# A fused linear-attention and squared-ReLU kernel: fill-in matmuls, another layout of the second weight matrix, and paired products instead of a doubled first product

## The chip, the cores and the metric

The kernel runs on one core of one Trainium2 chip. That core has a matmul engine (TensorE, "PE" in the profile, with its weight loads shown apart as "PEld"), three engines for elementwise work (VectorE or "DVE", ScalarE or "ACT", GpSimd or "POOL"), and SyncE ("SP"), which here only issues transfers. Sixteen DMA engines move the data. The metric is the device time of one launch in microseconds, lower is better.

## The reference, cut to what matters

Four batches, eight heads, 768 steps, head size 48. Per head a state of 48 x 48 decays by `w` each step and takes in `k` outer `v`; the result then goes through a two-layer block with a squared ReLU.

```python
for t in range(S):                      # S = 768, per batch and head
    cur = u * k[t] (outer) v[t]
    y[t] = r[t] @ (state + cur)
    state = w * state + k[t] (outer) v[t]
x = y as [3072, 384]                    # batch*step rows, head*48 columns
h = x @ w_in                            # [384, 2048]
g = max(h, 0) ** 2
out = g @ w_out                         # [2048, 384]
```

## The kernel before, in words

The 768 steps are cut into six chunks of 128. A **unit** is one chunk of one batch, 128 rows of `x` with all eight heads; there are 24, numbered chunk first, so unit `i` needs the state that unit `i - 4` left. For one unit the work is:

1. Three loads `rt`, `kt`, `vt` (`load`, L288), each 128 rows by 8 heads by 48 floats, in pieces of 192 bytes, on SP's queue.
2. `scale` (L311, DVE): `r` times a rising and `k` times a falling power of the decay, in bf16. `cast_v` (L315, ACT) casts `v`.
3. Both scaled tensors are transposed. For units 0 to 6 (`NPE = 7`) this is done by PE (`turn`, L331) and an ACT copy out of PSUM (`evict_rk`, L335); for the others by one DMA transpose on SP's queue (`turn_dma`, L320).
4. `at` (L348, PE): eight products q k^T of 64 x 128 operands, one per head. `mask` (L360, DVE, two a unit) keeps the part above the diagonal.
5. `rk`, `sums`, `diag_v` (L340, L368, L373, L382): the `u` term, and k^T v for the state. `state_add`, `state_decay`, `state_cast` (L390 to L402) carry the state.
6. `y_mm` and `evict_y` (L411 to L426): the unit's `y`. It is transposed to `xT`, by PE and ACT (`x_turn` L442, `evict_x` L446) for units 0 to 5 (`NPY = 6`) and by a DMA transpose on SP's queue (`x_dma`, L435) for the others.
7. `mm1` (L458): the first big product. A step makes one PSUM bank of 512 columns; a unit has four steps `s`, each with four blocks of 128 rows of `w_in` columns and three matmuls a block. `GROUPS` says over how many units a step reaches: for single units the moving operand has 128 columns, for a pair of units 256. In the kernel before units 0 to 7 and 20 to 23 are single and units 8 to 19 go in six pairs.
8. `relu` (L466, ACT) out of PSUM, then `square` on ACT (L473) or DVE (L475), dealt out in turn by `SQUARES = 'AMM'`: one on ACT, two on DVE.
9. `mm2` (L482): sixteen matmuls with 384 moving columns in four quarters, `evict_o` (L489, ACT), `store` (L519, SP). The last unit does it in two halves (L497, L508, L510, L515).

The weights come in eight transfers, four quarters `I0` to `I3` of `w_in` and four quarters `O0` to `O3` of `w_out` (`weights`, L294 to L302), on POOL's queue, cast to bf16 as they land. Ahead of each stands a small copy that waits until the `kt` load of a named unit has landed (list `front`). `columns` (L255, L256) loads `w` and `u` once more, one column a head pair; `spread_columns` (L268, PE) and `copy_columns` (L271, DVE) turn them, and POOL makes from them the `u` matrix (L274, L277) and the decay over a chunk (`end_columns`, L280, L282).

**Order.** Every engine's instruction order is written out by a planner (`Plan.run`, L42). Each step has an engine, an assumed cost, what it needs, and a rank; the planner steps through an assumed time, and gives a free engine the step of lowest rank whose needs, buffers and PSUM bank are there. What it produces is a fixed order for each engine; on the chip each engine takes its instructions in that order and waits at each for what it needs. `L1 = 7` and `L2 = 16` are the rank distances of `mm1` and `mm2` behind the attention work of the same unit (four ranks a unit). `room` and the banks' table limit buffers. `at_pair` and the branches on `PAIRED` are there in the kernel before but `PAIRED` is empty.

Of the kernel before, what the change touches and what calls it, by code (L numbers as in the profile page):

```python
# [10 lines left out]
BF16 = mybir.dt.bfloat16  # L11
# [138 lines left out]
def kernel(  # L150
# [11 lines left out]
    nc = tc.nc  # L162
# [10 lines left out]
    NPY = 6  # L173
    NPAD = 4
    SQUARES = 'AMM'
    GROUPS = (1,) * 8 + (2,) * 6 + (1,) * 4
    PAIRED = ()

    const = ctx.enter_context(tc.tile_pool(name="const", bufs=1))
    loads = ctx.enter_context(tc.tile_pool(name="loads", bufs=6))  # L180
    work = ctx.enter_context(tc.tile_pool(name="work", bufs=4))
    xpool = ctx.enter_context(tc.tile_pool(name="xpool", bufs=3))
    gpool = ctx.enter_context(tc.tile_pool(name="gpool", bufs=2))
    mpool = ctx.enter_context(tc.tile_pool(name="mpool", bufs=8))
# [21 lines left out]
    nc.scalar.preload_act_table_set("natural_log_exp_and_others")  # L206
    wu = const.tile([HP, 2, 2, 64], F32)
# [40 lines left out]
    w_in_sb = const.tile([128, NK, dff], BF16)  # L248
    w_out_sb = const.tile([128, NF, dm], BF16)
# [4 lines left out]
    def columns():  # L254
        nc.sync.dma_start(out=wu[:, 0, :, :D], in_=w.rearrange("(p o) d -> p o d", o=2))  # L255
        nc.sync.dma_start(out=wu[:, 1, :, :D], in_=u.rearrange("(p o) d -> p o d", o=2))  # L256
# [36 lines left out]
    def weights(i, q, which):  # L293
        nc.gpsimd.tensor_copy(gate, tiles[i]["kt"][:, 0, :1])  # L294
        if which == "I":
            sl = slice(q * dff // NQ, (q + 1) * dff // NQ)
            src = moe_w_in.rearrange("(ko ki) f -> ki ko f", ki=128)
            nc.gpsimd.dma_start(out=w_in_sb[:, :, sl], in_=src[:, :, sl])
        else:
            sl = slice(q * NF // NQ, (q + 1) * NF // NQ)  # L300
            src = moe_w_out.rearrange("(ko ki) f -> ki ko f", ki=128)
            nc.gpsimd.dma_start(out=w_out_sb[:, sl, :], in_=src[:, sl, :])  # L302
# [145 lines left out]
    def mm1(i, m, s):  # L448
        c, b = units[i]
        t = tiles[i]  # L450
        if b == 0 and s == 0:
            chunks[c]["g"] = gpool.tile([128, NF, B, C], BF16, name="g")
        t["h", s] = bank("h", i, s).rearrange("p (a u c) -> p a u c", u=m, c=C)
        for a in range(4 // m):
            f = s * (4 // m) + a
            for n in range(NK):
                turned = w_in_sb[:, n, f * 128 : (f + 1) * 128]
                nc.tensor.matmul(  # L458
                    out=t["h", s][:, a], lhsT=turned, rhs=chunks[c]["xT"][:, n, b : b + m, :],
                    start=(n == 0), stop=(n == NK - 1),  # L460
                )
# [15 lines left out]
    def mm2(i, q):  # L477
        t = tiles[i]
        if q == 0:
            t["o"] = bank("o", i)[:, :dm]  # L480
        for f in range(q * 4, q * 4 + 4):
            nc.tensor.matmul(  # L482
                out=t["o"], lhsT=chunks[units[i][0]]["g"][:, f, units[i][1], :], rhs=w_out_sb[:, f, :],
                start=(f == 0), stop=(f == NF - 1),
            )
# [5 lines left out]
    def mm2_half(i, n):  # L491
# [4 lines left out]
        for f in range(NF):  # L496
            nc.tensor.matmul(  # L497
                out=t["o"][:, sl], lhsT=chunks[units[i][0]]["g"][:, f, units[i][1], :], rhs=w_out_sb[:, f, sl],
                start=(f == 0), stop=(f == NF - 1), skip_group_check=True,
            )  # L500
# [23 lines left out]
    L1, L2 = 7, 16  # L524
# [11 lines left out]
    copy("wu", SP, 1.46, columns, rank=-99.75, move=(0.1, 16, 0.67, 0.1))  # L536
# [3 lines left out]
    add("wend", POOL, 2.6, end_columns, rank=-90, needs=["copied"])  # L540
    front = ['U0', 'U1', 'I0', 'U2', 'U3', 'I1', 'I2', 'I3', 'O0', 'O1', 'O2', 'O3', 'U4', 'U5']
    place = {what: -100 + n for n, what in enumerate(front)}
    seen = -1
    for what in front:
        if what[0] == "U":
            seen = int(what[1:])
        else:
            q = int(what[1])
            copy(
                (what[0], q), POOL, 1.0, do(weights, seen, q, what[0]), rank=place[what], move=((2.35, 98, 1.25, 0.0) if what[0] == "I" else (2.5, 78, 1.25, 0.0)),  # L550
                needs=[("kt", seen)], uses=[("ld", seen)],
            )
    for i in range(NU):
# [3 lines left out]
        rank = place.get(f"U{i}", a - 24)  # L557
# [5 lines left out]
        for x in range(2):  # L563
# [6 lines left out]
            ("vb", i), ACT, 0.405, do(cast_v, i), rank=a + 0.5, needs=[("vt", i), ("rkT", i) if i < 24 else ("scale", i, 1)],  # L570
# [17 lines left out]
        if i in PAIRED:  # L588
            add(
                ("at", i), PE, 0.645, do(at_pair, i), rank=a + 0, needs=[("rkT", i), ("rkT", i + 1)],  # L590
# [6 lines left out]
        for o in range(2):  # L597
# [5 lines left out]
            ("sums", i), PE, 0.275 if c < NCH - 1 else 0.105, do(sums, i), rank=a + (2.1 if c else 3.1),  # L603
# [3 lines left out]
        add(("dv", i), DVE, 0.465, do(diag_v, i), rank=a + 2.9, needs=[("sums", i), ("vb", i)], new=[("dv", i)], uses=[("s", i), ("vb", i)])  # L607
        if c < NCH - 1:
            add(
                ("sadd", i), DVE, 0.68, do(state_add, i), rank=a + (6 if c else 3.2),  # L610
                needs=[("sums", i), ("stb", before) if c else "wend"], uses=[("s", i)],
            )
            if c > 0:
                add(("sdec", i), DVE, 0.27, do(state_decay, i), rank=a + 4 + 4, needs=[("sadd", i)])
            add(
                ("stb", i), ACT, 0.71, do(state_cast, i), rank=a + 6 + 4,
# [18 lines left out]
    for m in GROUPS:  # L635
# [3 lines left out]
        for s in range(4 * m):  # L639
            rank = 4 * i + s + L1 + 4 * (m - 1)  # L640
# [12 lines left out]
        for j in range(i, i + m):  # L653
            a = 4 * j
            squares = [[("sq", i, s) for s in range(q * m, q * m + m)] for q in range(NQ)]
            if j < NU - 1:
                for q in range(NQ):
                    add(
                        ("m2", j, q), PE, 0.652, do(mm2, j, q), rank=a + q + L2 + 4 * (m - 1),
# [18 lines left out]
        ld=6, rkw=NPAD, g=2, rkT=4, vb=4, rk=4, am=8, dv=4, yb=4, xT=3, gr=8, osb=8,  # L678
    )
    for s in plan.run(room, dict(at=4, s=2, y=2, h=4, o=2), len(banks)):  # L680
# [32 lines left out]
```

## Time and profile before

| | |
|---|---|
| median of 3 runs | 183.15 us (180.97 to 185.44) |
| profiled execution, device time | 179.87 us |
| its span, first to last instruction | 178.1 us |
| busy: PE / DVE / ACT / POOL | 163.5 / 144.8 / 118.8 / 12.4 us |
| weight loads on PE, beside its matmuls | 125.2 us |
| DMA queue of SP, of POOL, as a share of 16 engines' span | 79.7% / 11.0% |

The profile's page gives busy time by engine, the span in 40 slices, the DMA queues, the chain of work that ended last, and the costliest groups of instructions. A busy PE isn't PE at its full rate, since matmuls overlap each other and their ends are modelled; the rate is read from how long a run of like matmuls takes in the timeline or the chain. The profiled execution is 3.3 us below the median of the runs shown.

### The profile page before, as it was taken

What the parts mean: (1) busy time and instruction counts of PE and PEld (TensorE: products, weight loads), DVE (VectorE), ACT (ScalarE), POOL (GpSimd) and SP (SyncE); (2) the same over time, 40 slices, a digit from 0 to 9 for tenths busy, and PEclk for the clock granted to TensorE, in tenths of its full rate; (3) what the DMA queues carried; (4) which work ended last, traced back from release to release, by engine and by line L of the source; (5) the groups of instructions that cost most, each with busy time, mean ns of one, the idle gap of its engine ahead of it and who ended that gap; (6) DMA issues with size and microseconds to landing.
All of it is one profiled execution on the core that took longest, in us unless ns stands there. A gap on an engine that the chain in (4) does not pass through costs nothing.

```text
span 178.1 us, 4914 instructions
## 1 busy us (share of the span) xinstructions
PE 163.5 (92%) x1982; PEld 125.2 (70%) x1982; DVE 144.8 (81%) x307; ACT 118.8 (67%) x240; POOL 12.4 (7%) x38
## 2 busy tenths in 40 slices
PE   2477889999999999999999999998999999999992
PEld 1356679886687886686786775784875788777771
DVE  4398998855899999999799999998998799762310
ACT  4546889987464965696694594694691897746620
POOL 3250950000000000000000000000000000000000
PEclk9999999999999999999999999999999999999999
DMA  5899999999955889999998899999999999811212
GB/s 116 161 184 202 171 200 187 184 202 184 129 107 95 155 158 197 118 207 213 137 206 180 167 193 159 207 188 135 222 199 137 216 163 208 235 47 26 90 62 70
DMA packets 107680, 28.56 MB, mean 160 GB/s; under 512 B 100873, under 2 KB 107658, under 8 KB 107658
## 3 DMA queue, kind: packets, MB, share of 16 engines
q1 hardware_dynamic: 103944, 25.11, 79.7%
q0 software_dynamic: 3712, 3.15, 11.0%
q8 instruction: 15, 0.25, 0.6%
q14 instruction: 7, 0.06, 0.1%
q10 hardware_dynamic: 2, 0.00, 0.0%
HBM read 20.45 MB, written 4.72 MB: 141 GB/s over the span
## 4 chain that ended last, share of the span: by engine, by line
PE 59%; DMA 21%; DVE 11%; ACT 3%; issue 2%; SPq 2%; ACTq 0%
PE bank L458 26%; PE bank L482 20%; DMA rkT<-rkw 12%; DMA xT<-yb 4%; PE bank L348 3%; DMA rt<-in_r_dram 3%; DVE rkw L311 3%; DMA kt<-in_k_dram 2%; PE bank L331 2%; DVE am L360 2%; DVE g L475 2%; PE bank L411 2%; DVE yb L426 2%; PE bank L497 1%; ACT rkT L335 1%
## 5 line engine op out<-in xcount | busy, mean ns | idle before, releaser
L458 PE MATMUL bank<-xT,w_in_sb 128*128 128x128 bf16 (+1 forms) x864 | 73.4, 238 | 0.3
L482 PE MATMUL bank<-w_out_sb,g 128*128 128x384 bf16 x368 | 68.3, 326 | 0.0
L466 ACT ACTIVATE gr<-bank 128x512 f32<-128x512 f32 x96 | 55.0, 594 | 18.9 <-PE bank L458 16.3
L458 PEld LDWEIGHTS <-w_in_sb 128*128 128x128 bf16 x864 | 61.2, 98 | 7.5 <-issue 0.5
L475 DVE TENSOR_TENSOR g<-gr 128x512 bf16<-128x512 f32 x64 | 43.1, 685 | 12.9 <-ACT gr L466 12.8
L482 PEld LDWEIGHTS <-g 128*128 128x128 bf16 x368 | 33.3, 98 | 18.1 <-DVE g L475 0.2
L360 DVE TENSOR_TENSOR am<-bank,smask 128x512 bf16<-128x512 f32 x48 | 31.7, 684 | 1.1 <-PE bank L348 0.7
L402 ACT CAST stb<-st 64x192 bf16<-64x192 f32 x40 | 13.9, 348 | 15.5 <-DVE st L396 14.6
L473 ACT ACTIVATE g<-gr 128x512 bf16<-128x512 f32 x32 | 20.1, 632 | 0.8
L489 ACT COPY osb<-bank 128x384 f32<-128x384 f32 x23 | 11.0, 478 | 8.4 <-PE bank L482 8.1
L311 DVE TENSOR_TENSOR rkw<-rt,wpos 128x384 bf16<-128x384 f32 x24 | 13.2, 550 | 3.0 <-ACT wpos L263 2.5
L426 DVE TENSOR_TENSOR yb<-bank,dv 128x384 bf16<-128x384 f32 x24 | 13.3, 553 | 1.3 <-PE bank L417 0.9
L311 DVE TENSOR_TENSOR rkw<-kt,wneg 128x384 bf16<-128x384 f32 x24 | 13.2, 551 | 1.3 <-DMA kt<-in_k_dram 1.3
L382 DVE TENSOR_TENSOR dv<-vb,bank 128x384 f32<-128x384 bf16 x24 | 13.1, 546 | 0.5 <-PE bank L373 0.5
L348 PE MATMUL bank<-rkT 64*128 64x128 bf16 x192 | 10.2, 229 | 3.6 <-ACT rkT L335 2.0
L340 DVE TENSOR_TENSOR rk<-rkT 128x512 bf16<-128x512 bf16 x24 | 10.1, 420 | 3.8 <-ACT rkT L335 1.9
L348 PEld LDWEIGHTS <-rkT 64*128 64x128 bf16 x192 | 5.8, 98 | 9.5 <-DMA rkT<-rkw 3.9
L315 ACT CAST vb<-vt 128x384 bf16<-128x384 f32 x24 | 12.2, 509 | 0.2
L335 ACT COPY rkT<-bank 128x512 bf16<-128x512 bf16 x14 | 8.2, 584 | 5.9 <-PE bank L331 5.6
L392 DVE TENSOR_TENSOR st<-bank,st 64x192 f32<-64x192 f32 x32 | 11.3, 352 | 0.2
L331 PE MATMUL bank<-identb,rkw 128*128 128x128 bf16 x56 | 6.7, 256 | 3.6 <-DVE rkw L311 1.8
L411 PEld LDWEIGHTS <-am 128*128 128x128 bf16 x192 | 8.4, 98 | 1.7 <-DVE am L360 0.3
(52 smaller groups left out, 90.2 us busy)
## 6 DMA issues: line engine op xcount, KB each, us to landing
rt<-in_r_dram SPq DMA_DIRECT2D x24, 192.0 KB, 3.1
kt<-in_k_dram SPq DMA_DIRECT2D x24, 192.0 KB, 3.8
vt<-in_v_dram SPq DMA_DIRECT2D x24, 192.0 KB, 4.0
out_dram<-osb SPq DMA_DIRECT2D x23, 192.0 KB, 2.9
w_in_sb<-in_moe_w_in_dram POOLq DMA_DIRECT2D x4, 384.0 KB, 7.6
w_out_sb<-in_moe_w_out_dram POOLq DMA_DIRECT2D x4, 384.0 KB, 13.8
xT<-yb SPq DMA_TRANSPOSE x18, 3.6
rkT<-rkw SPq DMA_TRANSPOSE x17, 3.7
```

The costliest lines, as they stand in the source:

```text
L311: nc.vector.tensor_tensor(t["rkw"][:, x, :, :, :D], pair(src), pair(wx), ALU.mult)
L315: nc.scalar.copy(tiles[i]["vb"], tiles[i]["vt"])
L348: nc.tensor.matmul(out=t["at"][o][:, p, :], lhsT=t["rkT"][sl, 1, p, :], rhs=t["rkT"][sl, 0, p, :], start=True, stop=True,)
L360: nc.vector.tensor_tensor(am, t["at"][o], smask.unsqueeze(1).to_broadcast([C, HP, C]), ALU.mult)
L382: nc.vector.tensor_tensor(t["dv"], t["vb"], t["d"].unsqueeze(2).to_broadcast([C, H, D]), ALU.mult)
L402: nc.scalar.copy(stb[b][sl, :, o * D : (o + 1) * D], st32[b][sl])
L426: nc.vector.tensor_tensor(t["yb"], t["y"], t["dv"].rearrange("p h d -> p (h d)"), ALU.add)
L458: nc.tensor.matmul(out=t["h", s][:, a], lhsT=turned, rhs=chunks[c]["xT"][:, n, b : b + m, :], start=(n == 0), stop=(n == NK - 1),)
L466: nc.scalar.activation(t["gr", s], t["h", s], AF.Relu)
L473: nc.scalar.activation(g, x, AF.Square)
L475: nc.vector.tensor_tensor(g, x, x, ALU.mult)
L482: nc.tensor.matmul(out=t["o"], lhsT=chunks[units[i][0]]["g"][:, f, units[i][1], :], rhs=w_out_sb[:, f, :], start=(f == 0), stop=(f == NF - 1),
```

## The change

- **Fill-in matmuls.** 50 matmuls of a constant tile (`warm`, 128 x 256, filled with ones by DVE) into one PSUM bank that nobody reads. They have the highest rank, so the planner puts them wherever it finds PE free, from the start; eight of them are due before the first real matmul.
- **`w_out` by four rows a partition.** A partition of a quarter of `w_out` now takes four consecutive rows (one run of 6,144 bytes) instead of four rows 128 apart (four runs of 1,536 bytes). So that the rows of `h` meet the right rows of `w_out`, `mm1` takes every fourth column of `w_in` as its weights instead of 128 neighbours. Both matrices are held as four tiles.
- **Pairs moved.** `GROUPS` is all single units; `PAIRED` makes `at` for two units at a time, units 8 to 23. The sixteen matmuls of a pair follow each other, once the transposes of both are there.
- **Dealing out.** `SQUARES = 'AM'`: ACT and DVE take turns with the squares (48 each instead of 32 and 64). `NPY = 10`: units 6 to 9 too have `xT` made by PE and ACT.
- **Queues and ranks.** The loads in `columns` go out on POOL's queue instead of SP's. `O0` moves ahead of `I2`. `state_add` of the first four units is put later (8 ranks instead of 3.2 behind its unit), that of the others earlier. `L1 = 9`. Buffers: 7 sets of loads for 6, 6 work buffers for 4, 5 buffers for 8 behind the big products, one bank for `y` instead of two, one for the fill.

```diff
-    NPY = 6
+    NPY = 10
-    SQUARES = 'AMM'
-    GROUPS = (1,) * 8 + (2,) * 6 + (1,) * 4
-    PAIRED = ()
+    SQUARES = 'AM'
+    GROUPS = (1,) * 24
+    PAIRED = (8, 10, 12, 14, 16, 18, 20, 22)
...
+    warm = const.tile([128, 256], BF16)
+    nc.vector.memset(warm, 1.0)
...
-    w_in_sb = const.tile([128, NK, dff], BF16)
-    w_out_sb = const.tile([128, NF, dm], BF16)
+    w_in_q = [const.tile([128, NK, dff // NQ], BF16, name=f"w_in_q{q}") for q in range(NQ)]
+    w_out_q = [const.tile([128, NF // NQ, dm], BF16, name=f"w_out_q{q}") for q in range(NQ)]
...
     def columns():
-        nc.sync.dma_start(out=wu[:, 0, :, :D], in_=w.rearrange("(p o) d -> p o d", o=2))
-        nc.sync.dma_start(out=wu[:, 1, :, :D], in_=u.rearrange("(p o) d -> p o d", o=2))
+        nc.gpsimd.dma_start(out=wu[:, 0, :, :D], in_=w.rearrange("(p o) d -> p o d", o=2))
+        nc.gpsimd.dma_start(out=wu[:, 1, :, :D], in_=u.rearrange("(p o) d -> p o d", o=2))
+
+    def fill():
+        nc.tensor.matmul(out=bank("fill")[:, :256], lhsT=warm[:, :128], rhs=warm, start=True, stop=True)
...
-            src = moe_w_out.rearrange("(ko ki) f -> ki ko f", ki=128)
-            nc.gpsimd.dma_start(out=w_out_sb[:, sl, :], in_=src[:, sl, :])
+            src = moe_w_out.rearrange("(q ki a) d -> q ki a d", q=NQ, a=NF // NQ)
+            nc.gpsimd.dma_start(out=w_out_q[q], in_=src[q])
...
-                turned = w_in_sb[:, n, f * 128 : (f + 1) * 128]
+                turned = w_in_q[f // 4][:, n, f % 4 :: 4]
...
-    L1, L2 = 7, 16
+    L1, L2 = 9, 16
...
-    copy("wu", SP, 1.46, columns, rank=-99.75, move=(0.1, 16, 0.67, 0.1))
+    copy("wu", POOL, 4.4, columns, rank=-99.75, move=(0.1, 16, 0.67, 0.1))
+    add("made", PE, 1.25, None, rank=-2e3)
+    for n in range(50):
+        add(
+            ("fill", n), PE, 0.215 if n < 16 else 0.108, fill, rank=1e3 + n, needs=[("fill", n - 1) if n else "made", "log" if n == 8 else None],
+            new=() if n else [("fill",)], uses=[("fill",)] if n else (),
+        )
...
-    front = ['U0', 'U1', 'I0', 'U2', 'U3', 'I1', 'I2', 'I3', 'O0', 'O1', 'O2', 'O3', 'U4', 'U5']
+    front = ['U0', 'U1', 'I0', 'U2', 'U3', 'I1', 'O0', 'I2', 'I3', 'O1', 'O2', 'O3', 'U4', 'U5']
...
-                add(("sdec", i), DVE, 0.27, do(state_decay, i), rank=a + 4 + 4, needs=[("sadd", i)])
+                add(("sdec", i), DVE, 0.27, do(state_decay, i), rank=a + 4 + 6, needs=[("sadd", i)])
...
-    for s in plan.run(room, dict(at=4, s=2, y=2, h=4, o=2), len(banks)):
+    for s in plan.run(room, dict(at=4, s=2, y=1, h=4, o=2, fill=1), len(banks)):
```

38 lines of the change are left out of this document (18 added, 20 removed).

## The prediction

> **What bounds the kernel now.** I read the page first, then the span in four stages, then the chain of work, then the timelines of the start. The page's span, busy times, two rows of slices and the chain's shares by engine:
>
> ```profile
> span 178.1 us, 4914 instructions
> PE 163.5 (92%) x1982; PEld 125.2 (70%) x1982; DVE 144.8 (81%) x307; ACT 118.8 (67%) x240; POOL 12.4 (7%) x38
> ...
> PE   2477889999999999999999999998999999999992
> ...
> DMA  5899999999955889999998899999999999811212
> ...
> q1 hardware_dynamic: 103944, 25.11, 79.7%
> q0 software_dynamic: 3712, 3.15, 11.0%
> ...
> PE 59%; DMA 21%; DVE 11%; ACT 3%; issue 2%; SPq 2%; ACTq 0%
> ```
>
> PE is full from the sixth slice on, but DMA is nearly as full until the 35th slice: the two queues hold 79.7% + 11.0% of 178.1 us, 161.5 us of sixteen engines. The view of busy time by stage (columns: stretch and length, then PE, weight loads, DVE, ACT, POOL, clock, DMA share, GB/s):
>
> ```profile
> 0.00:25.00 25.00, 15.81 (x186) 11.63 (x187) 19.04 (x54) 15.63 (x31) 12.43 (x38) 1.00 1.06 171
> 25.00:72.00 47.00, 46.98 (x666) 37.66 (x664) 40.91 (x85) 35.01 (x73) 0.00 (x0) 1.00 0.96 162
> 72.00:157.00 85.00, 83.11 (x941) 62.17 (x940) 78.95 (x161) 59.89 (x123) 0.00 (x0) 1.00 1.03 181
> 157.00:178.00 21.00, 17.63 (x196) 13.78 (x195) 5.89 (x10) 8.27 (x15) 0.00 (x0) 1.00 0.19 62
> ```
>
> So there are three places to gain in. The first 25 us leave PE idle for 25.00 - 15.81 = 9.2 us. From 25 to 72 us PE idles for 0.02 us: only fewer or shorter matmuls help there. From 72 to 157 us it idles for 1.9 us while DMA is full (1.03; shares above 1 come of two queues whose packets overlap). After that PE works off its backlog alone.
>
> Rates, from the chain (start, length, what):
>
> ```profile
> 35.20 1.34 PE bank L458 x24
> ...
> 48.96 0.17 PE bank L442 x3
> 49.40 0.65 PE bank L482 x4
> ...
> 106.15 5.45 DMA rkT<-rkw
> 111.65 0.40 PE bank L348 x8
> 112.04 0.76 PE bank L482 x4
> ...
> 118.61 4.91 DMA rkT<-rkw
> ...
> 126.66 3.28 PE bank L458 x30
> ```
>
> A first product of 128 columns takes 1.34/24 = 55.8 ns, one of 256 columns 3.28/30 = 109.3 ns. Four matmuls of the second product take 0.65 us, and 0.76 just behind an `at`: an `at` leaves a trace of 0.11 us in its successor.
>
> **The start.** PE's timeline, then SP's, POOL's and DVE's, and the time that quarters of `w_in` took to land:
>
> ```profile
> 13.35 0.61 PE L331 MATMUL bank<-identb,rkw 128*128 128x128 bf16 x4
> ...
> 16.95 1.46 PE L458 MATMUL bank<-xT,w_in_sb 128*128 128x128 bf16 x12
> ...
> 19.00 0.40 PE L331 MATMUL bank<-identb,rkw 128*128 128x128 bf16 x4
> 19.46 0.83 PE L458 MATMUL bank<-xT,w_in_sb 128*128 128x128 bf16 x12
> ...
> 24.96 2.17 PE L458 MATMUL bank<-xT,w_in_sb 128*128 128x128 bf16 x36
> ```
> ```profile
> 2.68 1.18 SPq L255 DMA_DIRECT2D wu<-in_w_dram  x1
> 3.91 0.63 SPq L256 DMA_DIRECT2D wu<-in_u_dram  x1
> ```
> ```profile
> 7.24 0.20 POOL L274 TENSOR_TENSOR cols<-cols 128x4 f32<-128x4 f32 x1 [4.94 <-DVE cols L271]
> ...
> 10.65 0.92 POOL L298 DMA_DIRECT2D w_in_sb<-in_moe_w_in_dram  x1
> 17.31 0.18 POOL L294 COPY gate<-kt 128x1 f32<-128x1 f32 x1 [5.75 <-DMA kt<-in_k_dram]
> 17.77 0.79 POOL L298 DMA_DIRECT2D w_in_sb<-in_moe_w_in_dram  x1 [0.28 <-issue]
> ```
> ```profile
> 11.51 0.73 DVE L390 TENSOR_TENSOR st<-bank,wend_c 64x192 f32<-64x192 f32 x2
> 12.27 0.56 DVE L426 TENSOR_TENSOR yb<-bank,dv 128x384 bf16<-128x384 f32 x1
> ```
> ```profile
> DMA to landing us min/median/max: 6.3/7.6/9.8
> ```
>
> Twelve first products take 1.46 us at 16.95 and 0.83 at 19.46, four transposes 0.61 and then 0.40: until about 18 us PE runs at half rate, though the granted clock's column says 1.00 there. The Trainium skill, "TensorE: Matmul & The Clock Gate", Part 1, has the clock halved until some 3.4 us of sustained work; by that rule the fills, begun near 1.3 us, open it before the first transposes, and the trace agrees as far as it goes: the rate doubles some 3 us after PE's work becomes dense.
>
> The first product starts at 16.95, and `w_in`'s first quarter, issued at 10.65 and landing 6.3 us or more later, is there no sooner than 16.95. The second quarter is issued at 17.77, because POOL waited 5.75 us for a `kt` load; it lands at 24.1 at the earliest, and PE's dense run begins at 24.96. So the weights and the loads ahead of them set the start.
>
> - Moving `columns` frees SP of 1.18 + 0.63 us, with gaps 1.9 us, ahead of unit 1's loads and all later ones; the second quarter's gate, bound to unit 3's `kt`, opens up to 1.9 us sooner, and the quarters behind it follow. On POOL the two transfers stand in its idle 4.94 us, ahead of the `u` matrix, the decay and `I0`. The price if they land later from there: PE's column transposes now stand ahead of unit 0's `turn`, DVE's copy ahead of unit 0's second `scale`, and each microsecond delays all of the first unit and `I0`. Bounds 0 and 1.9 us; I take 0 lost, as the columns are wanted only by 6 to 7 us.
> - `O0` ahead of `I2`: PE gets second products earlier and half of the first products 2 to 3 us later; with both at hand I count 0.
> - `state_add` of chunk 0 no longer stands before `yb`: 0.73 us of DVE off each of the first units' ways (it runs one unit later; unit 4 is the first that needs it). With the full clock, 0.6 us off the first product and 0.2 off each group of transposes. Part of this waits for the weights anyway: I take 1.1 us.
> - Fills: 50 matmuls of 256 columns, 50 x 0.109 = 5.5 us at full rate, 10.9 at half, against 9.2 us of idle PE. They stand in the order where the planner saw PE free, so I count 0; `warm`'s memset is in DVE's idle start.
>
> Start: 1.9 + 1.1 = **-3.0 us**, bounds 0 and -5.
>
> **Matmuls.** Groups by line with shapes kept apart:
>
> ```profile
> L458 PEld LDWEIGHTS <-w_in_sb 128*128 128x128 bf16 x864 | 61.2, 98 | 7.5 <-issue 0.5 <-DMA xT<-yb 0.4
> ...
> L475 DVE TENSOR_TENSOR g<-gr 128x512 bf16<-128x512 f32 x64 | 43.1, 685 | 12.9 <-ACT gr L466 12.8
> L458 PE MATMUL bank<-xT,w_in_sb 128*128 128x128 bf16 x576 | 37.5, 221 | 0.1
> L458 PE MATMUL bank<-xT,w_in_sb 128*128 128x256 bf16 x288 | 35.9, 273 | 0.2
> ...
> L473 ACT ACTIVATE g<-gr 128x512 bf16<-128x512 f32 x32 | 20.1, 632 | 0.8
> ...
> L446 ACT COPY xT<-bank 128x384 bf16<-128x384 bf16 x6 | 2.9, 477 | 1.3 <-PE bank L442 1.2
> ```
>
> - Six pairs of first products undone: 288 x 109.3 ns = 31.5 us become 576 x 55.8 = 32.1: **+0.7 us**.
> - Eight paired `at`: eight matmuls, two row halves side by side, would stream in 4 x 55.8 ns = 0.22 us, but an `at` costs 0.33 to 0.40 plus 0.11 in its successor, some 0.22 us too much. A pair pays that once: 8 x 0.22 = **-1.8 us** (bounds 0 and -2.3).
> - Four more units turned by PE: 4 x 0.17 = **+0.7 us**; ACT 4 x 0.48 = 1.9 us. SP loses four transposes.
> - Squares: 16 leave DVE (16 x 0.685 = 11 us less), and ACT gets 16 x 0.632 = 10.1. ACT comes to 118.8 + 10.1 + 1.9 = 131 us, DVE to 134; neither passes PE's 163.5. Cover for ACT in 25 to 72 us: 12 us idle, and it gets some 5.
> - `w_in` every fourth column: no row here has a strided weight load. From below 0: a load lasts 98 ns beside a matmul every 55.8 ns, so loads overlap already. From above, loads that no longer overlap: 1152 x (98 - 55.8) = +49 us. I take 0, the row it is nearest to, bf16 loads of the same 128 columns. The Trainium skill, "TensorE: Matmul & The Clock Gate", "Weight-path perf modes", lets the fast load take a column step up to 1,024, but says that it reads 32 bits at a time, which every fourth bf16 column doesn't fill: by the first statement the sum stays, by the second it would rise towards that +49; no run here shows it.
> - `w_out` in longer runs: fewer packets in the 11.0% queue, counted at 0 beyond the start.
>
> **Middle.** Of 1.9 us idle I take **-1.4**: one wait for transposes a pair instead of two, four transposes and DVE's 11 us less, 7 load sets. Bounds -1.9 and the pairing rival.
>
> Sum: -3.0 + 0.7 - 1.8 + 0.7 - 1.4 = **-4.8 us**. Against the profiled execution (178.1 of span and 1.8 around it, 179.87) that is 175.1. The runs shown have their median 3.3 us higher, so I forecast 183.15 - 4.8 = **178.4 us**, 175.9 to 181 by the bounds that I think likely.
>
> **Rivals.**
> - *DMA is the bound.* 161.5 us of packets and share 1.03 from 72 to 157 speak for it; 0.02 us of idle PE before 72 against. Then start and pairing gains are waited away in the middle: about 182.5.
> - *More goes.* If the start gives its 5 us and the runs come nearer the profile's 179.87, since the middle hangs less on DMA: 174.5.
> - *Pairing waits* (slower). Place: `at` of units 8 to 22. The first unit of a pair now waits for the second's `rkT`; transposes come (118.61 - 106.15)/2 = 6.2 us apart, and `L1` gives two of four ranks, 3.1 us, more lead. PE already waits 4.91 to 5.45 us transfers out there, so the backlog is thin; it decides from 0.6 us of new wait a pair, where 8 x 0.6 eats the 4.8. At 1.2 us a pair: 183.15 - 4.8 + 9.6 = 188.
> - *Strided weights* (slower): 178.4 + 49 = 227 at the full price; a tenth of it brings the time back to before.
> - *The fills don't do what they say*: the clock stays halved, they need 10.9 us where 9.2 are idle, and the 1.1 is lost: 178.4 + 1.7 + 1.1 = 181.2.
>
> **How the numbers follow.** Forecast 0.50, DMA 0.13, more 0.13, pairing 0.12, strided 0.08, fills 0.04. Two per cent, about what a measurement of this kernel can tell from no change (its runs spread 180.97 to 185.44), is 3.7 us: faster means below 179.5. Three quarters of the forecast's share lie there, with "more" 0.50; within 2% the rest of it, DMA and fills, 0.30; slower 0.20. The range from 174 to 188 leaves out the strided case and the ends of two others, 0.17.
>
> **What would show it.** In the profile after: twelve first products in about 0.83 us from the first on; dense PE from about 22 us; `at` as groups of 16 with some 0.67 us; first products still at 56 ns, their loads near 98; 72 to 157 us with under 1 us of idle PE. I am wrong if first products take over 60 ns, if idle PE stands ahead of the paired `at`, or if unit 0's `turn` comes after 7 us.

## The result, and the profile after

The changed kernel takes 180.66 us (median of 20 runs, 179.31 to 185.87), the kernel before 181.70 in 20 runs beside it on the same chips. The ratio is 0.993 (95% interval 0.9906 to 0.9960): about 1.2 us faster, where the forecast was 4.8. In most kernels here some runs come out longer, over 1.5% above the kernel's fastest; ratios leave them out (which leaves two of ten runs for a_act below, four of ten for a_true and one of four for a_sp), and where a profile fell on one, the text says "disturbed".

The profiled execution took 179.91 us with a span of 178.1, the same span as before (the copies of the last unit out of PSUM start at 174.37 us for 174.70). So the two traces show where a gain was made and where it was given back. The page after (busy times, slices, queues, the chain's shares):

```profile
span 178.1 us, 5590 instructions
PE 167.5 (94%) x2332; PEld 134.9 (76%) x2332; DVE 134.6 (76%) x292; ACT 127.6 (72%) x260; POOL 12.4 (7%) x40
...
PE   7799679999999999999998999998999999999991
...
DMA  6999999989479989899979896877998997322021
...
q1 hardware_dynamic: 102256, 24.72, 74.8%
q0 software_dynamic: 2240, 3.15, 9.8%
...
PE 68%; DVE 13%; DMA 10%; ACT 4%; issue 1%; POOL 1%; POOLq 0%; ACTq 0%
```

DVE has 10 us less, about as forecast (11); ACT has 9 more where 12 were forecast. The two queues hold 74.8% + 9.8% for 79.7% + 11.0%. PE's first slices are fuller, but partly with fills. In the chain DMA falls from 21% to 10%. Busy time by stage (columns as in the prediction):

```profile
0.00:25.00 25.00, 20.05 (x223) 14.37 (x224) 17.18 (x51) 13.92 (x28) 12.36 (x40) 1.00 1.14 178
25.00:72.00 47.00, 46.52 (x676) 38.09 (x674) 37.95 (x79) 38.87 (x81) 0.00 (x0) 1.00 1.00 173
72.00:157.00 85.00, 83.59 (x1229) 68.32 (x1228) 73.28 (x154) 64.14 (x133) 0.00 (x0) 1.00 0.86 170
157.00:178.00 21.00, 17.34 (x212) 14.07 (x209) 6.19 (x11) 10.67 (x20) 0.00 (x0) 1.00 0.19 59
```

From 72 to 157 us the transfers' share falls from 1.03 to 0.86 and PE's idle time from 1.89 to 85.00 - 83.59 = 1.41 us. The start is another matter. PE's timeline of the changed kernel (L261 fills, L273 the columns' transposes, L334 `turn`, L351 `at`, L461 first product):

```profile
1.19 1.89 PE L261 MATMUL bank<-warm 128*128 128x256 bf16 x8 [1.19 <-DVE warm L208]
...
6.40 0.24 PE L273 MATMUL bank<-ident,wu 4*128 4x4 f32 x1 [0.43 <-DMA wu<-in_w_dram]
7.24 0.26 PE L273 MATMUL bank<-ident,wu 4*128 4x4 f32 x1 [0.61 <-DMA wu<-in_u_dram]
...
7.84 0.63 PE L334 MATMUL bank<-identb,rkw 128*128 128x128 bf16 x4
...
11.02 1.00 PE L261 MATMUL bank<-warm 128*128 128x256 bf16 x4
11.96 0.40 PE L351 MATMUL bank<-rkT 64*128 64x128 bf16 x8
12.29 0.40 PE L334 MATMUL bank<-identb,rkw 128*128 128x128 bf16 x4
...
19.10 0.83 PE L461 MATMUL bank<-xT,w_in_q 128*128 128x128 bf16 x12
```

Unit 0's first `turn` starts at 7.84, the rate doubles only about 12 us (four transposes 0.63, then 0.40), and the first product starts at 19.10, 2.15 us later than before (16.95), not earlier. Ahead of the first `at` the fills run at half rate: four from 11.02 to 11.96, 0.24 us each. The chain of waits shows what stood first in line:

```profile
2.30 0.69 POOL wu L257
3.00 4.20 DMA wu<-in_u_dram
7.24 0.28 PE bank L273
7.63 1.50 DVE rkw L314 x3
...
9.73 1.07 PE bank L261 x5
10.80 0.43 PE bank L334 x4
11.23 0.80 PE bank L261 x4
```

The columns of `u`, a load of 1.5 KB, need 4.20 us from POOL's issue to landing. PE's order has its transpose ahead of unit 0's `turn`, and then nine fills stand between unit 0's last transposes and its `at`.

How far behind is PE after that? The view of busy time by stage, for the lines of the first and second product alone, counts the matmuls started by 33 and by 157 us. Before (L458, then L482):

```profile
0.00:33.00 33.00, 10.62 (x165) 1.00 1.10 175
0.00:157.00 157.00, 66.72 (x768) 1.00 1.01 174
...
0.00:157.00 157.00, 57.85 (x312) 1.00 1.01 174
```

and after (L461, then L485):

```profile
0.00:33.00 33.00, 7.80 (x122) 1.00 1.14 184
0.00:157.00 157.00, 68.39 (x1040) 1.00 0.94 172
...
0.00:33.00 33.00, 1.46 (x8) 1.00 1.14 184
0.00:157.00 157.00, 61.68 (x320) 1.00 0.94 172
```

Priced at 55.8 ns a single first product, 109.3 a double one and 162.5 a second product, the kernel before has 54.4 + 59.8 = 114.2 us of them left at 33 us, the changed one 57.5 + 58.5 = 116.0. It is 1.8 us behind, 0.7 of which is the dearer single products that the forecast counted elsewhere. At 157 us it is 0.4 us ahead (14.5 against 14.1). (The count leaves the attention work out. By 33 us both kernels have made ten `turn`, five `at` and the transposes of four `y`; in the rest of it the changed one is some 0.1 us ahead.) So the start cost 1.1 us where -3.0 was forecast, and the rest of the kernel won it back.

The groups by line with shapes kept apart, and a pair in PE's timeline:

```profile
L461 PE MATMUL bank<-xT,w_in_q 128*128 128x128 bf16 x1152 | 75.8, 219 | 1.4 <-DMA xT<-yb 1.4
...
L461 PEld LDWEIGHTS <-w_in_q 128*128 128x128 bf16 x1152 | 70.5, 114 | 6.9 <-DMA xT<-yb 1.3 <-issue 0.8
```
```profile
65.52 0.62 PE L351 MATMUL bank<-rkT 64*128 64x128 bf16 x16
66.07 0.26 PE L371 MATMUL bank<-uwb,rk 128*128 128x8 bf16 x4
```

A strided weight load lasts 114 ns for 98, but a first product's mean busy time is 219 ns for 221: the longer load is hidden. A pair's sixteen matmuls take 66.07 - 65.52 = 0.55 us. If they leave a trace of 0.11 once, as a lone `at` did before, two `at` apart, at least 0.33 and 0.11 each, cost 0.22 us more, as forecast. No wait stands ahead of the pair: PE's only waits from 72 to 157 us are two for `xT`, 1.4 us in all.

### The profile page after: what moved, and what is told of

Same layout as the page of the kernel before. It is cut to its first block, busy times and chain, and to the rows that moved or that the text cites. A ratio compares the mean times of both kernels' runs of the same rounds, so it can differ in the third digit from the quotient of the medians.

```text
span 178.1 us, 5590 instructions
## 1 busy us (share of the span) xinstructions
PE 167.5 (94%) x2332; PEld 134.9 (76%) x2332; DVE 134.6 (76%) x292; ACT 127.6 (72%) x260; POOL 12.4 (7%) x40
## 3 DMA queue, kind: packets, MB, share of 16 engines
q1 hardware_dynamic: 102256, 24.72, 74.8%
## 4 chain that ended last, share of the span: by engine, by line
PE 68%; DVE 13%; DMA 10%; ACT 4%; issue 1%; POOL 1%; POOLq 0%; ACTq 0%
PE bank L461 28%; PE bank L485 26%; DMA xT<-yb 5%; DVE am L363 4%; DMA rkT<-rkw 3%; PE bank L351 2%; DMA wu<-in_u_dram 2%; DVE rkw L314 2%; PE bank L414 2%; DVE yb L429 2%; PE bank L261 2%; ACT rkT L338 2%; PE bank L334 2%; PE bank L500 1%; PE bank L420 1%
## 5 line engine op out<-in xcount | busy, mean ns | idle before, releaser
L461 PE MATMUL bank<-xT,w_in_q 128*128 128x128 bf16 x1152 | 75.8, 219 | 1.4 <-DMA xT<-yb 1.4
L461 PEld LDWEIGHTS <-w_in_q 128*128 128x128 bf16 x1152 | 70.5, 114 | 6.9 <-DMA xT<-yb 1.3
L485 PE MATMUL bank<-w_out_q,g 128*128 128x384 bf16 x368 | 70.6, 326 | 0.0
L478 DVE TENSOR_TENSOR g<-gr 128x512 bf16<-128x512 f32 x48 | 32.9, 688 | 24.1 <-ACT gr L469 24.1
L485 PEld LDWEIGHTS <-g 128*128 128x128 bf16 x368 | 32.8, 98 | 15.7
L363 DVE TENSOR_TENSOR am<-bank,smask 128x512 bf16<-128x512 f32 x48 | 31.0, 684 | 3.8 <-PE bank L351 3.8
L476 ACT ACTIVATE g<-gr 128x512 bf16<-128x512 f32 x48 | 30.4, 636 | 1.0
L261 PE MATMUL bank<-warm 128*128 128x256 bf16 x50 | 10.4, 347 | 1.2 <-DVE warm L208 1.2
L414 PE MATMUL bank<-vb,am 128*128 128x48 bf16 x192 | 8.8, 183 | 0.0
L414 PEld LDWEIGHTS <-am 128*128 128x128 bf16 x192 | 7.7, 96 | 1.4
L351 PE MATMUL bank<-rkT 64*128 64x128 bf16 x192 | 8.1, 218 | 0.1
```

The lines of the kernel that those rows point to most:

```text
L261: nc.tensor.matmul(out=bank("fill")[:, :256], lhsT=warm[:, :128], rhs=warm, start=True, stop=True)
L363: nc.vector.tensor_tensor(am, t["at"][o], smask.unsqueeze(1).to_broadcast([C, HP, C]), ALU.mult)
L414: nc.tensor.matmul(out=y[:, 2 * p + o, :], lhsT=t[f"am{o}"][:, p, :], rhs=t["vb"][:, 2 * p + o, :], start=(o == 0 and p == 0), stop=c == 0 ...
L461: nc.tensor.matmul(out=t["h", s][:, a], lhsT=turned, rhs=chunks[c]["xT"][:, n, b : b + m, :], start=(n == 0), stop=(n == NK - 1),)
L476: nc.scalar.activation(g, x, AF.Square)
L478: nc.vector.tensor_tensor(g, x, x, ALU.mult)
```

## The experiments

Three theories of the start's loss: **A**, the late columns ahead of unit 0's `turn`; **B**, fills at half rate ahead of the first `at`; **D**, the weights, issued some 3 us earlier, hold back the loads of units 4 and 5. A rival, **C**, is that the landing of `w_in`'s first quarter alone sets the first product. All ratios are to the kernel before, run beside each kernel on the same chip.

### The columns' queue, and the fills

```diff
 a_sp           (copy("wu", SP, 1.46, ...) and nc.sync for both loads)
 a_act          (copy("wu", ACT, 1.1, ..., rank=-1e3, needs=["w0"], ...) and nc.scalar for both)
 a_nofill       (the 50 fills, "made" and the fill's bank taken out)
 a_act_nofill   (both of the last two)
```

> The changed kernel with the two loads of `columns` back on SP's queue, all else kept. Theory A (the columns come late from POOL's queue and hold up unit 0): unit 0's first `turn` comes at about 6.2 us instead of 7.84, the first product about 1.5 us sooner than 19.10, the time about 1.5 us shorter, ratio to the kernel before 0.985. Theory B (the fills hold up unit 0, because they run at half rate): first `at` still near 11.5 us, ratio stays at 0.993. Rival C (the weights' landing alone sets the first product): first product not sooner than 18 us, ratio 0.993.

> The changed kernel without the fills and their tile, columns still on POOL. Theory A: unit 0's first `turn` still after 7.2 us; the ratio stays near 0.993 or rises towards 1.00, because PE then runs at half rate until some 19 us. Theory B: the first `at` comes near 10.3 us instead of 11.96, the first product 1 to 2 us sooner, ratio 0.985. Rival C: first product where the first quarter of `w_in` lands, 18 us or a little sooner, ratio 0.993.

> The changed kernel with the two loads of `columns` on ACT's queue, behind the logarithm, with the fills. Theory A: as with SP's queue or a little better, since SP's loads stay 1.9 us ahead: ratio 0.980 to 0.985. Theory B: 0.993. Rival C: 0.993.

> Columns on ACT's queue and no fills. If A and B both hold their gains add: first `turn` near 6.2 us, first `at` near 8.6 us as in the kernel before, first product near 16.5 us, ratio 0.975 to 0.98. If the half rate without fills costs what I forecast (1.1 us), it is no better than with the fills on ACT's queue, 0.985. Rival C: 0.99.

| | median us | ratio | first `turn` / `at` / product at |
|---|---|---|---|
| after | 180.66 | 0.993 (0.991 to 0.996) | 7.84 / 11.96 / 19.10 |
| a_sp | 185.78 | none, disturbed | 6.18 / 9.89 / 17.48 |
| a_nofill | 181.38 | 0.997 (0.992 to 1.002) | 7.51 / 10.05 / 17.96 |
| a_act | 182.98 | 0.990 (0.982 to 0.997) | 6.89 / 10.99 / 18.14 |
| a_act_nofill | 180.52 | 0.994 (0.989 to 0.998) | 7.27 / 9.81 / 17.43 |

Each edit brings the first product 1.0 to 1.7 us earlier, so A and B are both at work there; the intervals of the three ratios all overlap that of the changed kernel. C doesn't bind in the changed kernel: the first quarter, issued at 11.23, landed 6.6 us later, at 17.8, and the first product came at 19.10. Where the earlier start may go is seen in PE's timeline of the kernel with the columns back on SP (disturbed):

```profile
27.07 0.61 PE L334 MATMUL bank<-identb,rkw 128*128 128x128 bf16 x4 [3.56 <-DVE rkw L314]
...
28.90 2.75 PE L461 MATMUL bank<-xT,w_in_q 128*128 128x128 bf16 x24
```

PE waits 3.56 us for unit 4's `scale`, whose `kt` is late, and then runs at half rate again (24 products in 2.75 us, where the changed kernel needs 1.51). With the columns on ACT's queue the same wait is 2.20 us (disturbed too). This is what D says, but D isn't shown: a_nofill and a_act_nofill, undisturbed, start 1.1 and 1.7 us earlier as well and have no such wait (PE's longest from 18 to 36 us is under 0.9 us). In a_nofill it is the rate that uses the earlier start up: the half rate lasts until some 26 us, and by 33 us 97 first products are done where the changed kernel has 122. Twelve first products in its timeline (0.83 us at full rate):

```profile
25.26 1.48 PE L456 MATMUL bank<-xT,w_in_q 128*128 128x128 bf16 x12
```

### The planner's costs set right, and the weights put behind unit 4's `kt`

```diff
 a_true
-    copy("wu", POOL, 4.4, columns, ...)
+    copy("wu", POOL, 5.4, columns, ...)
-            ("fill", n), PE, 0.215 if n < 16 else 0.108, ...
+            ("fill", n), PE, 0.215 if n < 30 else 0.108, ...
 a_true_g4 and b_true_g4 (one kernel, on two chips): a_true and
-    front = ['U0', 'U1', 'I0', 'U2', 'U3', 'I1', 'O0', 'I2', 'I3', 'O1', 'O2', 'O3', 'U4', 'U5']
+    front = ['U0', 'U1', 'I0', 'U2', 'U3', 'I1', 'U4', 'O0', 'I2', 'I3', 'O1', 'O2', 'O3', 'U5']
 b_nofill_g4:    the same without fills
 a_sp_nofill_g4: a_sp, without fills, with that front
```

> The changed kernel with two of the planner's assumptions set to what its trace shows: the columns land about a microsecond later (5.4 for 4.4), and 30 fills instead of 16 take 0.215 us. Nothing else is edited; unit 0's `turn` then stands ahead of the column transposes, fewer fills stand before the first `at`, and the first quarter of `w_in` is issued before the decay's seven operations. Theories A and B together (order written for times that the chip doesn't keep): first `turn` near 6.2 us, first `at` near 9 us for 11.96, first product near 17.5 us for 19.10, ratio 0.985. Theory D (transfers in the first 40 us are the limit, so what the queue of SP gains is lost to weights that come sooner): first product sooner but unit 4's loads not, PE idles ahead of unit 4's `turn`, ratio 0.99 to 0.995.

> As a_true, and the second to eighth weight quarters but one (`O0`, `I2`, `I3`, `O1` to `O3`) wait for unit 4's `kt` instead of unit 3's. Theory D: unit 4's `scale` comes by 22 us, no idle PE of over 1 us ahead of its `turn`, against a later `O0` (28 us or more); the time 1 us below a_true, ratio 0.98 to 0.985. Theories A and B alone: no better than a_true, or worse by the later weights, 0.99.

> The changed kernel without the fills, with the columns back on SP's queue and the weights held as in a_true_g4: the start nearly that of the kernel before, the rest (pairs, single first products, strided weights, squares, four more turns by PE) as changed. If the start is where the forecast went wrong and the middle as forecast (2 us or so less), this comes to -2 us: ratio 0.988. If the middle gave less than forecast, 0.995 or more.

> a_true_g4 again, with more rounds, as the base of the three runs beside it: ratio 0.985 to 0.99, a span near 176.3 us, dense first products from 15.5 us, no idle PE of over 1 us after 21 us.

> b_true_g4 without the fills, in an order that fits its times. What a full clock at the start is worth: by my term (0.6 us of first product and 0.2 us a group of transposes, part of it hidden) 1.1 us, so ratio 0.006 higher than b_true_g4. Rival: the DVE and the transfers set the start, and the clock is worth nothing: same ratio. Second rival: the fills cost more than they bring, ratio lower.

| | median us | ratio |
|---|---|---|
| a_true | 179.61 | 0.987 (0.983 to 0.992) |
| a_true_g4 | 178.25 | 0.989 (0.981 to 0.996) |
| b_true_g4 | 178.08 | 0.986 (0.980 to 0.991) |
| a_sp_nofill_g4 | 180.43 | 0.999 (0.996 to 1.002) |
| b_nofill_g4 | 180.63 | 0.996 (0.992 to 1.001) |

With a load of 5.4 us instead of 4.4 the planner puts unit 0's `turn` ahead of the columns, and with 30 fills at half rate fewer of them ahead of `at`. PE's timeline of a_true_g4:

```profile
6.19 0.63 PE L334 MATMUL bank<-identb,rkw 128*128 128x128 bf16 x4
...
9.30 0.61 PE L351 MATMUL bank<-rkT 64*128 64x128 bf16 x8
9.84 0.40 PE L334 MATMUL bank<-identb,rkw 128*128 128x128 bf16 x4
...
15.52 0.86 PE L461 MATMUL bank<-xT,w_in_q 128*128 128x128 bf16 x12
```

The first product comes 3.6 us earlier than in the changed kernel, 1.4 earlier than before: half of the forecast's 3.0. The weight load of that product waits 0.21 us for `w_in`'s first quarter, so here C begins to bind. In a_true, without the new gate, PE waits 1.87 us for unit 4's `vt` at 32.13 (disturbed). With the gate that wait is gone, and the span is 176.3 us for 178.5 (disturbed). The medians say 1.4 us better, but the two ratios of one batch overlap (0.987 and 0.989), so the gate's own worth isn't settled. The kernel with the two costs set right and the gate beats the kernel before on two chips; against the changed kernel's 0.993 its ratios are 0.005 and 0.008 lower, with intervals that still touch. The fills, once they stand right, are worth 0.9964 - 0.9856 = 0.011, some 2 us; in the changed kernel taking them out changed nothing that the intervals tell (0.993 and 0.997).

a_sp_nofill_g4 has neither late columns nor fills, and its first product comes at 17.10, near the 16.95 of the kernel before. If only the start had gone wrong, it was to be 2 us faster than the kernel before; it is level with it (0.999). So the rest of the change fell short of its forecast too, unless the gate takes something back there, which no run separates.

Nor does the repaired start give what was forecast. At 33 us a_true_g4 has 144 first and 8 second products done, 0.1 us more than the kernel before once the 0.7 us of dearer single products are set aside, and some 0.5 us more of attention work: 0.6 us ahead, not 3.0, with a first product 1.4 us sooner. From 12 to 24 us DVE is busy for 11.38 of 12 us before, 11.42 in the changed kernel and 11.84 in a_true_g4, so an earlier PE finds DVE nearly full there. No run relieves DVE in that stretch; how much of the missing gain it holds back stays open.

### Each of the two edits alone, with the gate

```diff
 c_g4:      the changed kernel, only the front of a_true_g4
 c_wu_g4:   c_g4 with 5.4 for 4.4 in "wu"
 c_fill_g4: c_g4 with n < 30 for n < 16 in the fills' cost
```

> The changed kernel with one edit: the weights' transfers behind w_in's two column quarters wait until unit 4's k is issued. The start's own order (columns ahead of unit 0's turn, fills at half rate ahead of the first turned unit) is untouched. If the late columns and the half-rate fills set the loss (theory A with B), the first turn stays at 7.8 us, the first turned unit at about 12.0, the first product at about 19.1, and the ratio stays at 0.99 to 0.995. If it was mainly the weights in front of unit 4's loads (theory D), the wait for unit 4 goes and the ratio falls to that of the kernel with right planner constants and the same gate, 0.986 to 0.989.

> As the kernel with the gate on unit 4's k alone, and the planner told that the columns' first loads take 5.4 for 4.4, so that unit 0's first turn stands ahead of the columns on TensorE; the fills stay counted at 0.108 us from the 16th. Theory A (columns in front of the turn): the first turn at about 6.2 us, the first turned unit by 10 or 10.5, and most of the gain, ratio 0.986 to 0.99. Theory B (fills at half rate in front of the first turned unit): the first turn is earlier but the first turned unit stays behind 10.5, ratio 0.99 to 0.995.

> As the kernel with the gate on unit 4's k alone, and the planner told that the first 30 fills take 0.215 us and not 16; the columns stay in front of unit 0's turn. Theory B: fewer fills lie in front of the first turned unit, which comes at about 10.5 to 11 for 12.0, ratio 0.986 to 0.99. Theory A: the turn stays at 7.8 us, the first turned unit at 11.5 or later, ratio 0.99 to 0.995.

Lead is the work in first and second products done by that time beyond c_g4's, from the counts and prices used above.

| | median us | ratio | `turn` / `at` / product at | lead at 33 us | lead at 157 us |
|---|---|---|---|---|---|
| c_g4 | 180.49 | 0.998 (0.994 to 1.003) | 7.86 / 12.03 / 19.62 | 0 | 0 |
| c_fill_g4 | 180.69 | 0.999 (0.994 to 1.004) | 8.07 / 11.17 / 18.70 | 0.7 | -0.8 |
| c_wu_g4 | 181.80 | 1.008 (1.002 to 1.014) | 6.18 / 9.32 / 15.18 | 2.3 | 0.7 |
| a_true_g4 | 178.25 | 0.989 (0.981 to 0.996) | 6.19 / 9.30 / 15.52 | 2.7 | 1.7 |

So the loss of the start is mostly A: the columns ahead of the `turn` are worth 2.3 of 2.7 us of lead, the fills' cost 0.7. (All leads are over c_g4, which the gate puts 1.5 us behind the changed kernel at 33 us and 0.3 at 157; over the changed kernel a_true_g4 leads by 1.2 and 1.4.) What I expected of the whole time was wrong, though: c_wu_g4 starts as early as a_true_g4 and yet ends behind the kernel before. The middle takes back 1.0 to 1.6 us of any lead, and c_wu_g4 loses more. Its timeline shows a part of it:

```profile
19.31 0.38 PE L334 MATMUL bank<-identb,rkw 128*128 128x128 bf16 x4 [0.77 <-ACT rkT L338]
...
22.01 1.44 PE L461 MATMUL bank<-xT,w_in_q 128*128 128x128 bf16 x12 [0.32 <-ACT xT L449]
```

Its fills are used up by 15 us, waits follow, and the rate halves (twelve products in 1.44 us). The granted clock's row of its page shows it, with a 6 in the sixth slice (the last slice lies behind PE's last matmul):

```profile
PEclk9999969999999999999999999999999999999996
```

This isn't one run's accident: the mean granted clock is 0.981 to 0.992 in eight of its ten runs, and 0.995 to 1.000 in all runs of a_true_g4 and c_g4. At 33 us it is 0.4 us behind a_true_g4, at 157 us 1.0 (a wait of 1.1 us for one `rkT` lies between), and at the end 2.6 by the spans (178.9 against 176.3). Of these, 1.05 us are there when the copies of the last unit out of PSUM start (173.59 against 172.54). The other 1.5 us lie behind PE's work, between there and the end; what makes them stays open. Nor is the gate a gain by itself: c_g4 is no faster than the changed kernel.

### `w_out` by rows

```diff
 b_contig_g4:  b_true_g4 with the old layouts, and the planner's old cost of a quarter of `w_out`
-            src = moe_w_out.rearrange("(q ki a) d -> q ki a d", ...)
+            src = moe_w_out.rearrange("(q a ki) d -> q ki a d", ...)
-                turned = w_in_q[f // 4][:, n, f % 4 :: 4]
+                turned = w_in_q[f // 4][:, n, f % 4 * 128 : (f % 4 + 1) * 128]
-                ... else (2.05, 78, 1.25, 0.0)
+                ... else (2.5, 78, 1.25, 0.0)
 before_rows:  the kernel before with the new layouts, one tensor for each matrix
+                turned = w_in_sb[:, n, f // 4 * 512 + f % 4 : f // 4 * 512 + 512 : 4]
 before_q:     the kernel before with four tensors for each matrix, old layouts
 before_qrows: before_q with the new layouts
```

> b_true_g4 with both weight matrices laid out as in the kernel before: `w_in` columns side by side, `w_out` in runs of 1,536 bytes. My terms were 0 for the strided loads and 0 for the longer runs: same ratio as b_true_g4 within 0.003, weight loads of the first product near 98 ns instead of 114 and first products 56 ns apart in both. If the stride holds PE up, faster than b_true_g4; if the longer runs relieve the transfers, slower by up to 0.5 us a quarter, 2 us.

> The kernel before with one part of the change: w_out is loaded by four rows a partition, and w_in's columns are read with a step of four to match. By the prediction's term (0 for the longer runs, 0 for strided weight loads) the ratio is 0.997 to 1.003. If w_out's shorter packet time relieves the DMA engines in the kernel before as it seems to in the changed one (about 10 us of 16 engines falling to 8), the ratio is 0.988 to 0.995. If strided weight loads cost something, it is above 1.003.

> The kernel before with w_out by four rows a partition, w_in's columns read with a step of four, and both weights kept in four tensors of a quarter each, as in the changed kernel. If the 7 per cent that the same edit cost with one tensor for each weight came from the wait that the strided reads put on the next quarter's loads (theory E), w_in's four quarters are issued without a wait for TensorE, as in the kernel before, and the ratio falls to 0.985 to 1.003: 0.997 to 1.003 by the prediction's term (0), 0.985 to 0.995 if the longer runs relieve the transfers as they seemed to in the changed kernel. If strided weight loads themselves are dear (theory F), the ratio stays above 1.03.

> The kernel before with both weights kept in four tensors of a quarter each and nothing else: the order on every engine and every transfer is that of the kernel before, so 0.997 to 1.003 by all theories. It is the base against which the longer runs of w_out are read.

| | median us | ratio |
|---|---|---|
| b_contig_g4 (beside b_true_g4, 178.08) | 179.74 | 0.999 (0.995 to 1.002) |
| before_rows | 193.59 | 1.071 (1.060 to 1.082) |
| before_q | 181.15 | 1.003 (0.998 to 1.008) |
| before_qrows | 182.94 | 1.015 (1.006 to 1.023) |

In the repaired kernel the old layouts cost 0.9985 - 0.9856 = 0.013, some 2 us by ratios and 1.0 us by the undisturbed spans (177.3 against a_true_g4's 176.3). But with the planner's old cost PE's order differs too, from some 28 us on, so this isn't the worth of the longer runs alone. In the kernel before the new layouts seem to cost: 1.0149 - 1.0032 = 0.012, with intervals that just overlap. I expected neither. before_rows was a surprise that explains a piece of the change; POOL's timeline:

```profile
18.53 0.79 POOL L298 DMA_DIRECT2D w_in_sb<-in_moe_w_in_dram  x1 [3.63 <-PE bank L442]
...
25.30 0.78 POOL L298 DMA_DIRECT2D w_in_sb<-in_moe_w_in_dram  x1 [5.78 <-PE bank L458]
```

`w_in`'s second and third quarter are issued at 18.53 and 25.30 because POOL waits there for PE. In one tensor, the strided reads of a quarter are evidently put ahead of the next quarter's write (theory E); with four tensors (before_qrows) the quarters go out at 15.00 to 16.82 with no wait for PE, and most of the 7% is gone. That the strided weight loads themselves cost those 7% (theory F) is out with it. So the change's four tensors aren't decoration: without them its strided reads would hold up its own weights. Where before_qrows may lose the rest is seen at SP, here in before_q and then in before_qrows (disturbed):

```profile
16.67 1.52 SPq L288 DMA_DIRECT2D rt<-in_r_dram  x1
```
```profile
16.61 4.80 SPq L288 DMA_DIRECT2D rt<-in_r_dram  x1
```

With long runs of `w_out` behind it, the same load's issue is held 4.80 us for 1.52, and PE waits 2.67 us for an `rk` at 26.57, a wait that before_q doesn't have. The longer runs shorten the queue's total (page: 9.6% of 183.6 us against 10.9% of 178.9). That their packets stand in the way of the units' short loads is a guess: the two kernels' orders differ in nothing else, but the only profile of before_qrows is disturbed, and no undisturbed one shows the hold-up.

### Pairs and squares

```diff
 a_nopair:  the changed kernel
-    PAIRED = (8, 10, 12, 14, 16, 18, 20, 22)
+    PAIRED = ()
 b_amm_g4:  b_true_g4
-    SQUARES = 'AM'
+    SQUARES = 'AMM'
```

> The changed kernel with `PAIRED` empty: each `at` of units 8 to 23 alone. My term for the pairs was 1.8 us: each lone `at` again costs 0.33 and 0.11 in its successor, and the ratio rises from 0.993 to 1.003. Rival: the pairs gain nothing because PE waits for transposes anyway: 0.993.

> b_true_g4 with `SQUARES = 'AMM'` as in the kernel before (32 squares on ACT, 64 on DVE). I had counted DVE's relief and ACT's load as hidden, apart from some of the middle: same ratio within 0.003. If ACT bounds PE in the first 48 us (it is 10.9 of 12 us busy there in the changed kernel), faster; if DVE's relief mattered, slower by 1 us or more.

a_nopair: 183.11 us, ratio 1.003 (0.998 to 1.008), span 178.7. Against the changed kernel's 0.993 the pairs are worth 0.009, 1.7 us (0.6 by the spans). b_amm_g4: 178.30 us, ratio 0.989 (0.984 to 0.994): dealing the squares out otherwise changes nothing that can be measured.

## Why the prediction was wrong

The forecast was -4.8 us, the change gave -1.2. By the prediction's own steps:

- **Start, -3.0: the step that failed.** Measured: +1.1 us at 33 us. Five assumptions in it broke.
  - "I take 0 lost, as the columns are wanted only by 6 to 7 us." The prediction named the price of late columns and set it at 0. They landed at 7.2, and the order written for an assumed 4.4 us had them ahead of unit 0's `turn`. Putting the `turn` first is worth 2.3 us of lead at 33 us.
  - "They stand in the order where the planner saw PE free, so I count 0", of the fills. The planner took 0.108 us for all but sixteen; on the chip they took about 0.24 until 12 us, so the place wasn't free: 0.7 us of lead. The prediction had a rival for it, but with a chance of 0.04 and as a clock that never opens; what happened is that it opened late.
  - "0.73 us of DVE off each of the first units' ways." Only unit 0 is rid of it. From unit 1 on, the `state_add` put off from the unit before stands directly ahead of `yb`, and PE waits there. DVE in the chain after, then PE's timeline:

```profile
17.92 0.36 DVE st L393
18.31 0.56 DVE yb L429
```
```profile
18.92 0.34 PE L445 MATMUL bank<-identb,yb 128*128 128x128 bf16 x3 [0.92 <-DVE yb L429]
...
23.09 0.34 PE L445 MATMUL bank<-identb,yb 128*128 128x128 bf16 x3 [1.31 <-DVE yb L429]
```

  These two are PE's longest waits from 18 to 36 us.
  - "So the weights and the loads ahead of them set the start." The second quarter did go out sooner, at 15.00 for 17.77: 2.8 us where up to 1.9 were forecast. PE's dense run still begins only at 25.48 for 24.96. The sum counted DVE in that one `state_add` alone; it is nearly full from 12 to 24 us.
  - "With gaps 1.9 us, ahead of unit 1's loads and all later ones", for the columns off SP's queue. SP's issues of `rt` in the changed kernel:

```profile
2.72 0.72 SPq L293 DMA_DIRECT2D rt<-in_r_dram  x1
...
8.69 1.17 SPq L293 DMA_DIRECT2D rt<-in_r_dram  x1
...
17.72 1.17 SPq L293 DMA_DIRECT2D rt<-in_r_dram  x1
18.93 4.37 SPq L293 DMA_DIRECT2D kt<-in_k_dram  x1
23.35 10.24 SPq L293 DMA_DIRECT2D vt<-in_v_dram  x1
```

  The same three loads went out at 4.59, 9.26 and 17.72 before: 1.87 us gained for unit 1, 0.57 for unit 3, 0 for unit 5. SP's later issues last longer (10.24 us at unit 5's `vt`, 2.55 before), so their count doesn't set when they go out. I priced a queue by its issue slots; that the transfers in flight hold them is my reading, which no run isolates.
- **Single first products +0.7, four more `turn` +0.7**: no run isolates them; first products keep their pace (24 in the chain's 1.34 us before, 48 in the 2.69 us from 29.86 to 32.55 in the timeline after, 56.0 ns).
- **Pairs -1.8**: 1.7 us by ratios, 0.6 by spans. No pair waits for its second unit: the rival "pairing waits" is out.
- **Squares 0, strided weight loads 0**: held. The Trainium skill, "TensorE: Matmul & The Clock Gate", "Weight-path perf modes", allows its fast weight load a column step up to 1,024; the load of 114 ns for 98 with a step of four, and the unchanged pace, agree with that and not with a full loss.
- **`w_out` runs 0**: not settled. Together with the planner's cost, 1 to 2 us gained in the repaired kernel; in the kernel before some 2 us lost by ratios whose intervals overlap.
- **Middle -1.4**: PE's idle time there fell by 0.5 us only. The waits for transposes that remain are two of `xT`, and the middle takes back 1.0 to 1.6 us of an earlier start, which the prediction gave only to the DMA rival. With the transfers' share down to 0.86 there, what takes it back isn't shown. The prediction also put shares above 1 down to two queues; from 72 to 157 us SP's queue makes 1.02 of the 1.03 alone.

With the start at +1.1, the rest of the forecast's terms (-1.8) and 0.9 us less in the middle, the sum is +0.2; the two profiled spans are equal, and the ratio says -1.2. In the repaired kernel, where the order of columns and fills fits their times, the median is 2.4 to 2.9 us below the kernel before. So those two assumptions explain part of the miss; the rest of the start, and the middle, stay open.

## What to carry to other kernels

An order written out from assumed costs turns each wrong cost into a wait: before trusting "it stands where the engine is free", compare the assumed duration with the one in the trace at that time, at the clock of that time. Taking two issues off a queue speeds up only what waits for issue slots; look at how long later issues on that queue last before counting the gain further on. And an earlier start is worth what the other engines and the loads let through: here a first product 1.4 us sooner left PE 0.6 us ahead at 33 us, with DVE nearly full in between.

## What the runs showed of the hardware that I hadn't expected

- Fills from 1.19 us on didn't bring the full rate before 12 us, with PE waiting 0.43 and 0.61 us for the columns at 6.4 and 7.2. In a_true_g4, without those two waits, transposes took 0.40 us by 9.84. In a_true, whose PE order and times are the same up to there, they still took 0.60 at 9.83 and the rate doubled at about 11 us: it varies from run to run, and waits alone don't explain it. The Trainium skill, "TensorE: Matmul & The Clock Gate", Part 1, gives some 3.4 us of sustained work; PE had been at work for longer than that in all three. The granted clock's column showed 1.00 all along in this stretch.
- The half rate comes back after waits: after 3.56 us of idle PE (a_sp, disturbed), after 1.72 us (b_true_g4, disturbed: 24 first products in 26.91 - 24.96 = 1.95 us, where they take 1.34 at the full rate), and in c_wu_g4 at 22.01 with no single wait above 0.8 us. This the granted clock's column does show: 0.72 from 24 to 36 us in a_sp, 0.86 there in b_true_g4, 0.92 from 12 to 24 us and 0.94 from 24 to 36 us in c_wu_g4. The half rate of the start it doesn't show.
- A load of 1.5 KB took 4.20 us to land from POOL's queue. From ACT's queue (a_act_nofill) the columns' transposes started at 5.83 and 7.07: the second was hardly earlier than from POOL's (7.24).
